# One product placed before the last of seven, first-MoE down products of two chunks in one PSUM sum, input low parts on VectorE

## The chip, the core and the metric

The kernel runs on one core of a Trainium2 chip. The metric is the device time of one execution in microseconds. Before the change the median of three runs is 1148.57 us (1141.18 to 1149.47). The execution that was profiled took 1143.19 us; its span, from the first to the last instruction, is 1141.2 us.

## What is computed

Three stages follow one another on 1536 tokens of 512 numbers (2 batches of 768 tokens, 8 heads of 64):

```
mask  = argmax(q_n . c_n) == argmax(k_n . c_n)               # cluster attention, per batch and head
x     = softmax(where(mask, q k^T / 8, -1e9)) v              # (1536, 512)
x     = (silu(x w_gate) * (x w_val)) w_out                   # first MoE: 512 -> 1536 -> 512
out   = sum over e in 0..3 of p[:, e] * (relu(x w1[e]) w2[e])  # second MoE: 512 -> 1024 -> 512, four experts
```

All of it is float32 in the reference. The kernel keeps the precision by splitting each matmul operand into a high part in the type fp32r and the float32 remainder, its low part, also in fp32r. A product of two such operands is three matmuls: high by high, high by low, low by high.

## The kernel before

**Attention** comes first (function `attention`, lines 173 to 535). Its time is not touched by the change.

**Chunks.** Both MoE stages walk over the hidden dimension in chunks of 256 columns (`FC` = 2 blocks `f` of 128). The first MoE has 6 chunks (`NC1`), the second 16 (`E2 * NC2`, four per expert). Tokens are taken in three blocks `tb` of 512.

**First MoE.** `up(key)` makes, for each block and each `f`, a gate and a value product of 12 matmuls each (`proj`, line 162), then SiLU, product, high part (ScalarE) and low part (VectorE) of the hidden tile `hh`, `hl`. `down(prev)` follows one chunk behind: 12 tiles (3 `tb` by 4 `d`) of 6 matmuls each (line 773), and after every tile VectorE adds the tile into the accumulator `acc1` in SBUF (lines 776 and 778). So the order on TensorE is up 0, up 1, down 0, up 2, down 1, and so on; down 5 runs when the second MoE begins. In the last down, ScalarE writes the high part `xh` of the second MoE's input (line 781) and GpSimd writes its low part `xl` (line 782).

**Second MoE.** `up_fast(key)` computes the first two token blocks by a scheme of seven products instead of eight (Strassen's, in Winograd's form), each product 6 matmuls (line 682), and the third token block directly, two products `g` of 12 matmuls (line 162). Some of the seven are added up in the same PSUM bank: the bank `pa` holds a product, VectorE (`add`, line 702) reads it, and then the last product is accumulated on top of it, so that the matmuls of the last product wait for VectorE's read. The sums of input blocks that the scheme needs, `x_sum(0)` to `x_sum(3)`, are made once, by the generator `x_sums` (lines 635, 636, 641), which is advanced in pieces (`side["x"]`) between the tiles of the last first-MoE down and inside the first `up_fast`. The results go through `fin` (lines 695, 696): ReLU and high part on ScalarE, low part on VectorE. `down(key)` then runs 12 tiles of 6 matmuls, taking the token tiles of block 2 first, then 1, then 0 (line 801), with the hidden tile as the stationary operand; VectorE scales by `pn` and adds to `acc2` (line 808). One chunk of the second MoE is thus 66 matmuls up and 72 down.

**Order of the work.** The whole order is written out by hand (`tc.manual_schedule()`): each engine executes its instructions in program order. Weight preparation (split into high and low parts, `w_steps`) is cut into small steps; `stage(i)` chooses the pieces for the coming chunk and `step()`, called at fixed places in `up`, `up_fast` (through `fin`) and `down`, issues some of them. A step loads the next piece through SyncE's DMA queue (`w_load`; two raw buffers), and for the second MoE four GpSimd operations make sums of weight blocks (lines 133 to 136).

**PSUM.** The up products rotate through two banks tagged `a` and two tagged `b`, the down tiles through three.

Of the kernel before, what the change touches and what calls it, by code (L numbers as in the profile page):

```python
# [7 lines left out]
F32 = mybir.dt.float32  # L8
# [5 lines left out]
ALU = mybir.AluOpType  # L14
# [21 lines left out]
def tile_cluster_attention_moe(ctx, tc, qk, vt, cent, consts, wm1, wm2, probs, out):  # L36
# [28 lines left out]
    def add_pieces(k, part):  # L65
        n = 512 if k[0] == 1 else 1024
        base, size = (0, UP[k[0]]) if part == "u" else (UP[k[0]], DN)
        pieces.extend((k, part, o, base + o) for o in range(0, size, n))

    add_pieces(chunks[0], "u")  # L70
    for i, k in enumerate(chunks):
        if k[0] == 2:
            add_pieces(k, "d")
        if i + 1 < len(chunks):
            add_pieces(chunks[i + 1], "u")
        if k[0] == 1:
            add_pieces(k, "d")
    loaded = []
    nload = [0]

# [74 lines left out]
    def proj(key, ps, base, f, tb, ks=range(4)):  # L155

        wh, wl = wt[key, "u"]
        for k in ks:
            o = base + k * FC * 128 + f * 128
            xs = (xh[:, k, tb * 512:(tb + 1) * 512], xl[:, k, tb * 512:(tb + 1) * 512])  # L160
            for m, (w, x) in enumerate(((wh, xs[0]), (wh, xs[1]), (wl, xs[0]))):
                T.matmul(out=ps, lhsT=w[:, o:o + 128], rhs=x, start=(k == 0 and m == 0), stop=(k == 3 and m == 2))  # L162
# [419 lines left out]
    def moe():  # L582
# [2 lines left out]
        ap_ = ctx.enter_context(tc.tile_pool(name="acc", bufs=1))  # L585
        tp = ctx.enter_context(tc.tile_pool(name="tp", bufs=3))
        ps_u = ctx.enter_context(tc.tile_pool(name="ps_u", bufs=2, space=PSUM))
        first_stage = ExitStack()
        hp1 = first_stage.enter_context(tc.tile_pool(name="hp1", bufs=1))
        acc = ap_.tile([128, 4 * NT], F32, tag="acc", name="acc")  # L590
        acc1 = acc.rearrange("p (d n) -> p d n", d=4)
        acc2 = acc.rearrange("p (t n) -> p t n", n=DM)
# [1 line left out]

        def stage(i):

            k = chunks[i]
            nxt = chunks[i + 1:i + 2]
            want = [(x, "u") for x in nxt]
            if k[0] == 2 or nxt[0][0] != k[0]:  # L600
                want.append((k, "d"))
            if k[0] == 1 and i:
                want.append((chunks[i - 1], "d"))
            todo = [x for x in pieces if x[:2] in want]

            def work():
                for x in todo:
                    yield from w_steps(*x[:3])

            side["work"] = work()  # L610
            side["steps"] = sum(5 if x[0][0] == 1 else 4 if x[1] == "u" else 2 for x in todo)
            side["calls"] = 7 if i == 0 else 20 if k[0] == 1 else 14

        def step():
            n = -(-side["steps"] // max(side["calls"], 1))
# [38 lines left out]

        def x_sum(i):

            if i == 0:
                return [(xh[:, j, 512:1024], xl[:, j, 512:1024]) for j in range(2)]
            return [(x_t[0][:, i - 1, j], x_t[1][:, i - 1, j]) for j in range(2)]

        def up_fast(key):

# [4 lines left out]
            def A_(f, k):  # L667
                return [(2 * k + i) * FC * 128 + f * 128 for i in range(2)]
# [7 lines left out]
            def T_(n):  # L676
                return x_sum(n - 1)
# [7 lines left out]
            def bank(tag):  # L685
                return ps_u.tile([128, 512], F32, tag=tag, name="p" + tag)
# [6 lines left out]
            def fin(f, tb, c):  # L693
                sl = slice(tb * 512, (tb + 1) * 512)
                A.activation(out=hh[:, f, sl], in_=c, func=ACTF.Relu)
                V.scalar_tensor_tensor(out=hl[:, f, sl], in0=c, scalar=0.0, in1=hh[:, f, sl].bitcast(F32),
                                       op0=ALU.max, op1=ALU.subtract)
                step()

            def add(f, tb, ps, t):  # L700
                c = tp.tile([128, 512], F32, tag="sg", name="sg")
                V.tensor_tensor(out=c, in0=ps, in1=t, op=ALU.add)  # L702
                fin(f, tb, c)
# [6 lines left out]
            for _ in range(2):  # L710
                next(side["x"], None)
            add(0, 0, pb, m1)
            for f in range(2):
                g = bank("b")
                proj(key, g, 0, f, 2)
                fin(f, 2, g)
                for _ in range(3):
                    next(side["x"], None)
            pc = bank("a")
            prod(pc, S_(1), T_(1), True)  # L720
            m5 = snap(pc)
# [3 lines left out]
            add(0, 1, pc, u2)  # L725
            prod(pa, S_(3), T_(3), False)
            add(1, 1, pa, m5)
            prod(pa, A_(1, 1), T_(4), False)
            fin(1, 0, pa)
            wt.pop((key, "u"))  # L730
# [6 lines left out]
        def up(key):  # L737
# [20 lines left out]
                    step()  # L758
            wt.pop((key, "u"))

        def down(key):
            hh, hl = h_t.pop(key)
            wh, wl = wt.pop((key, "d"))
            if key[0] == 1:
                first, last = key[1] == 0, key[1] == NC1 - 1
                for tb in range(3):
                    sl = slice(tb * 512, (tb + 1) * 512)
                    for d in range(4):
                        ps = down_banks[0].tile([128, 512], F32, tag="d", name="pd")
                        for f in range(FC):  # L770
                            o = f * DM + d * 128
                            for m, (w, x) in enumerate(((wh, hh), (wh, hl), (wl, hh))):
                                T.matmul(out=ps, lhsT=w[:, o:o + 128], rhs=x[:, f, sl],  # L773
                                         start=(f == 0 and m == 0), stop=(f == FC - 1 and m == 2))
                        if first:
                            V.tensor_copy(out=acc1[:, d, sl], in_=ps)
                        else:
                            V.tensor_tensor(out=acc1[:, d, sl], in0=ps, in1=acc1[:, d, sl], op=ALU.add)
                        if last:
                            if tb != 1 or d > 1:  # L780
                                A.copy(out=xh[:, d, sl], in_=acc1[:, d, sl])  # L781
                                G.tensor_tensor(out=xl[:, d, sl], in0=acc1[:, d, sl], in1=xh[:, d, sl].bitcast(F32), op=ALU.subtract)  # L782
                            if tb:
                                if (tb, d) == (1, 1):
                                    side["x"] = x_sums()
                                for _ in range((1 if tb == 1 else 2) if (tb, d) != (1, 0) else 0):
                                    next(side["x"], None)
                        else:
                            step()
            else:  # L790
                e = key[1] // NC2
                first, last = key[1] == 0, key[1] == E2 * NC2 - 1
                cuts = [(tb * 4 + t, slice(0, DM)) for tb in (2, 1, 0) for t in range(4)]
                if last:
                    cuts[-1:] = [(cuts[-1][0], slice(i * DM // 2, (i + 1) * DM // 2)) for i in range(2)]
                for t, cs in cuts:
                    ps = down_banks[0].tile([128, 512], F32, tag="d", name="pd")[:, cs]
                    for f in range(FC):
                        ts_ = slice(t * 128, (t + 1) * 128)
                        for m, (x, w) in enumerate(((hh, wh), (hh, wl), (hl, wh))):  # L800
                            T.matmul(out=ps, lhsT=x[:, f, ts_], rhs=w[:, f * DM + cs.start:f * DM + cs.stop],  # L801
                                     start=(f == 0 and m == 0), stop=(f == FC - 1 and m == 2))
                    pe = pn[:, t, e:e + 1]
                    y = acc2[:, t, cs]
                    if first:
                        V.tensor_scalar(out=y, in0=ps, scalar1=pe, scalar2=None, op0=ALU.mult)
                    else:
                        V.scalar_tensor_tensor(out=y, in0=ps, scalar=pe, in1=y, op0=ALU.mult, op1=ALU.add)  # L808
                    if last:
                        SY.dma_start(out=out[t * 128:(t + 1) * 128, cs], in_=y)  # L810
                    step()

        prev = None
        for i, k in enumerate(chunks):
            stage(i)
            if k[0] == 2:
                if prev is not None:
                    first_stage.close()
                    sp = ctx.enter_context(tc.tile_pool(name="sp", bufs=1))
                    x_t.extend(sp.tile([128, 3, 2, 512], F32R, name="t" + x) for x in "hl")  # L820
                    down(prev)
                    prev = None
                up_fast(k)
                down(k)
                for _ in side["work"]:
                    pass
                continue
            up(k)
            if prev is not None:
                down(prev)  # L830
            for _ in side["work"]:
                pass
            prev = k

    with tc.manual_schedule():
        attention()
# [39 lines left out]
```

## Time and profile before

| what | value |
|---|---|
| median of three runs | 1148.57 us |
| the profiled execution, and its span | 1143.19 us, 1141.2 us |
| TensorE busy, share of the span | 1071.9 us, 94% |
| VectorE, ScalarE, GpSimd busy | 751.1, 480.2, 203.4 us |
| mean granted TensorE clock | 0.978 of 2.4 GHz |
| chain that ended last | TensorE 83%, VectorE 11%, ScalarE 3% |

The chain is followed back from the last instruction, at each step to what released it. A busy TensorE is not TensorE at its peak, since the ends of matmuls are modelled (0.39 us each, while they start 0.23 us apart); the rate is read from start to start. Idle time of an engine that nobody waits for costs nothing. Attention takes the first 304 us, the first MoE runs to 586.54 us, and the second MoE from there to the end.

### The profile page before, as it was taken

Reading aid. Unit: us, or ns where it says so; the run is one execution under the profiler, and the core shown is the slowest. Engines: PE = TensorE matmul, PEld = TensorE weight load, DVE = VectorE, ACT = ScalarE, POOL = GpSimd, SP = SyncE. Lnnn points to the kernel's source line nnn. Section 1 sums busy time; section 2 is a strip of 40 time slices with the busy share of each in tenths; the row PEclk is TensorE's granted clock in tenths of the full one; section 3 lists DMA queues with packets and bytes.
Section 4 is the critical chain, followed back from the end, with each engine's and each line's share of the span. In section 5 each row is a group of like instructions: output and inputs, shape, how many; then the busy total and the mean of one; then the engine's idle time right before and its main releaser. Section 6 shows DMA issues by size and latency. Waiting matters only on the chain.

```text
span 1141.2 us, 13780 instructions
## 1 busy us (share of the span) xinstructions
PE 1071.9 (94%) x5178; PEld 898.6 (79%) x5178; DVE 751.1 (66%) x1301; ACT 480.2 (42%) x962; POOL 203.4 (18%) x192
## 2 busy tenths in 40 slices
PE   5999999999999999999989999999999999999998
PEld 3898888888888888888867777877777877777776
DVE  4798999898567566675686555555555555555554
ACT  2697888999544324243241222212222122222211
POOL 3435655442000000001051110111110111110000
PEclk9798999999999999999999999999999999999999
DMA  9666676731122121221101111001111001111002
GB/s 230 150 166 150 152 166 160 183 72 43 52 74 74 56 74 57 59 72 55 56 1 37 37 38 37 19 19 37 38 38 37 19 19 37 38 37 37 19 1 111
DMA packets 36594, 78.59 MB, mean 69 GB/s; under 512 B 16272, under 2 KB 18800, under 8 KB 36528
## 3 DMA queue, kind: packets, MB, share of 16 engines
q1 hardware_dynamic: 20256, 55.70, 17.0%
q0 software_dynamic: 16272, 22.02, 9.1%
q8 instruction: 40, 0.66, 0.2%
q14 instruction: 26, 0.21, 0.1%
HBM read 70.39 MB, written 3.19 MB: 64 GB/s over the span
## 4 chain that ended last, share of the span: by engine, by line
PE 83%; DVE 11%; ACT 3%; issue 1%; DMA 1%; SPq 0%; DVEq 0%; ACTq 0%
PE pd L801 23%; PE pb L162 16%; PE pa L682 10%; PE pd L773 8%; PE pa L162 8%; PE ps L324 5%; PE ps L300 2%; PE ps L301 2%; PE pv L342 2%; PE pv L341 2%; DVE sg L702 2%; DVE lo L332 2%; PE pb L682 2%; DVE junk L306 1%; PE pc L243 1%
## 5 line engine op out<-in xcount | busy, mean ns | idle before, releaser
L808 DVE SCALAR_TENSOR_TENSOR acc<-pd,pn,acc 128x512 f32<-128x512 f32 (+1 forms) x181 | 134.8, 747 | 93.0 <-PE pd L801 92.1
L801 PE MATMUL pd<-wdh,hh 128*128 128x512 f32 (+1 forms) x386 | 150.7, 390 | 0.0
L801 PE MATMUL pd<-wdl,hh 128*128 128x512 f32 (+1 forms) x386 | 150.5, 390 | 0.0
L801 PE MATMUL pd<-wdh,hl 128*128 128x512 f32 (+1 forms) x386 | 150.0, 389 | 0.0
L690 ACT COPY snap<-pa 128x512 f32<-128x512 f32 x48 | 28.2, 588 | 268.0 <-PE pa L682 268.0
L133 POOL TENSOR_TENSOR ws<-wraw 128x256 f32<-128x256 f32 x16 | 13.6, 852 | 649.6 <-DMA wraw<-in_wm 283.8
L332 DVE TENSOR_TENSOR lo<-ps,hi 128x384 fp32r<-128x384 f32 x192 | 101.4, 551 | 13.5 <-ACT hi L326 12.4
L162 PE MATMUL pb<-xl,wuh 128*128 128x512 f32 x264 | 103.9, 394 | 1.5 <-POOL xl L782 1.5
L162 PE MATMUL pb<-xh,wuh 128*128 128x512 f32 x264 | 103.7, 393 | 1.6 <-ACT xh L781 1.1
L324 PE MATMUL ps<-ident,P 128*128 128x128 f32 x576 | 91.5, 287 | 13.8 <-DVE lo L332 13.5
L162 PE MATMUL pb<-xh,wul 128*128 128x512 f32 x264 | 103.6, 392 | 0.0
L306 DVE CUSTOM_DVE_ANT_1 junk<-ps,zero 128x768 bf16<-128x768 f32 x96 | 90.9, 947 | 13.2 <-PE ps L301 12.5
L326 ACT CAST hi<-ps 128x384 fp32r<-128x384 f32 x192 | 85.8, 483 | 28.0 <-PE ps L324 25.8
L318 ACT ACTIVATE P<-ps,nm 128x768 f32<-128x768 f32 x96 | 87.3, 909 | 14.5 <-DVE nm L306 13.4
L324 PEld LDWEIGHTS ps<-ident,P 128*128 128x128 f32 x576 | 69.6, 146 | 28.7 <-DVE lo L332 21.8
L801 PEld LDWEIGHTS pd<-wdh,hh 128*128 128x128 f32 x386 | 73.3, 190 | 15.3
L801 PEld LDWEIGHTS pd<-wdl,hh 128*128 128x128 f32 x386 | 73.1, 189 | 15.3
L801 PEld LDWEIGHTS pd<-wdh,hl 128*128 128x128 f32 x386 | 73.0, 189 | 15.2
L341 PE MATMUL pv<-hi,vs 128*128 128x384 f32 x192 | 74.2, 386 | 0.0
L300 PE MATMUL ps<-t 80*128 80x384 f32 x192 | 72.3, 377 | 0.5 <-ACT P L318 0.4
L682 PE MATMUL pa<-th,wuh 128*128 128x512 f32 x96 | 40.9, 426 | 32.8 <-DVE sg L702 32.8
L301 PE MATMUL ps<-t 128*128 128x384 f32 x192 | 67.8, 353 | 0.0
(159 smaller groups left out, 2316.5 us busy)
## 6 DMA issues: line engine op xcount, KB each, us to landing
wraw<-in_wm SPq DMA_DIRECT2D x68, 512.0 KB, 3.7
t<-in_qk POOLq DMA_DIRECT2D x15, 768.0 KB, 5.5
t<-in_qk POOLq DMA_DIRECT2D x18, 384.0 KB, 6.8
raw<-in_qk SPq DMA_DIRECT2D x32, 192.0 KB, 7.0
x<-x SPq DMA_DIRECT2D x21, 192.0 KB, 4.8
vs<-in_vt POOLq DMA_DIRECT2D x16, 192.0 KB, 3.8
vraw<-in_vt SPq DMA_DIRECT2D x16, 192.0 KB, 3.8
R<-rd SPq DMA_DIRECT2D x16, 192.0 KB, 3.5
```

Source lines behind the costliest of these rows:

```text
L162: T.matmul(out=ps, lhsT=w[:, o:o + 128], rhs=x, start=(k == 0 and m == 0), stop=(k == 3 and m == 2))
L300: T.matmul(out=ps, lhsT=t2[:, 0, qs], rhs=t2[:, 1, ks], start=True, stop=False)
L301: T.matmul(out=ps, lhsT=t1[:, 0, qs], rhs=t1[:, 1, ks], start=False, stop=True)
L306: V.tensor_tensor_reduce(out=junk.rearrange("p (c n) -> p c n", c=2), in0=S_t[n][:, :, :384], in1=zero1.rearrange("p (o n) -> p o n", o=1) ...
L318: A.activation(out=P_t[n].rearrange("p (c n) -> p c n", c=2), in_=S_t.pop(n)[:, :, :384], func=ACTF.Exp, scale=0.125, bias=nm_t.pop(n), ac ...
L324: T.transpose(ps[:, i * 128:(i + 1) * 128], P_t[3 * u + i][:, j * 128:(j + 1) * 128], ident)
L332: V.tensor_tensor(out=lo, in0=ps, in1=hi.bitcast(F32), op=ALU.subtract)
L341: T.matmul(out=pv_t[u], lhsT=lhsT, rhs=hi, start=(j == 0), stop=False)
L682: T.matmul(out=ps, lhsT=w[:, o:o + 128], rhs=r, start=first and i == 0 and m == 0, stop=i == 1 and m == 2, skip_group_check=not first)
L773: T.matmul(out=ps, lhsT=w[:, o:o + 128], rhs=x[:, f, sl], start=(f == 0 and m == 0), stop=(f == FC - 1 and m == 2))
L801: T.matmul(out=ps, lhsT=x[:, f, ts_], rhs=w[:, f * DM + cs.start:f * DM + cs.stop], start=(f == 0 and m == 0), stop=(f == FC - 1 and m == 2))
L808: V.scalar_tensor_tensor(out=y, in0=ps, scalar=pe, in1=y, op0=ALU.mult, op1=ALU.add)
```

## The change

There are three parts.

1. In `up_fast`, the third block's product for `f` = 1 is issued after the sixth of the seven products and its `add`, and before the last. Before, both products of the third block stood together ahead of the products of sums.
2. In the first MoE, the down products of two chunks (0 and 1, 2 and 3, 4 and 5) are done together, by `down_pair`, after the second one's `up`: one PSUM tile takes 12 matmuls, 6 of each chunk, and VectorE adds once per tile. The order of the weight pieces and the number of steps per call follow.
3. In the last pair the low parts `xl` are made by VectorE, one tile behind, instead of by GpSimd. The input sums are stored in the hidden tile of chunk 4, which is read block by block, instead of in a tile of their own, and the generator is advanced at somewhat other places.

```
@@ order of weight pieces
         if k[0] == 2:
             add_pieces(k, "d")
+        elif k[1] % 2:
+            add_pieces(chunks[i - 1], "d")
+            add_pieces(k, "d")
         if i + 1 < len(chunks):
             add_pieces(chunks[i + 1], "u")
-        if k[0] == 1:
-            add_pieces(k, "d")
@@ stage
-            nxt = chunks[i + 1:i + 2]
-            want = [(x, "u") for x in nxt]
-            if k[0] == 2 or nxt[0][0] != k[0]:
+            want = [(x, "u") for x in chunks[i + 1:i + 2]]
+            if k[0] == 2:
                 want.append((k, "d"))
-            if k[0] == 1 and i:
-                want.append((chunks[i - 1], "d"))
+            elif k[1] % 2:
+                want += [(x, "d") for x in chunks[i - 1:i + 1]]
...
-            side["calls"] = 7 if i == 0 else 20 if k[0] == 1 else 14
+            side["calls"] = 7 if i == 0 else 14 if k[0] == 2 else 10 if k[1] % 2 == 0 or k[1] == NC1 - 1 else 20
@@ x_sum
-            return [(x_t[0][:, i - 1, j], x_t[1][:, i - 1, j]) for j in range(2)]
+            tb = (None, 1, 0, 2)[i]
+            return [[t[:, j, tb * 512:(tb + 1) * 512] for t in x_t] for j in range(2)]
@@ up_fast
             add(0, 0, pb, m1)
-            for f in range(2):
-                g = bank("b")
-                proj(key, g, 0, f, 2)
-                fin(f, 2, g)
-                for _ in range(3):
-                    next(side["x"], None)
+            g = bank("b")
+            proj(key, g, 0, 0, 2)
+            fin(0, 2, g)
+            for _ in range(2):
+                next(side["x"], None)
             pc = bank("a")
             prod(pc, S_(1), T_(1), True)
...
             prod(pa, S_(3), T_(3), False)
             add(1, 1, pa, m5)
+            g = bank("b")
+            proj(key, g, 0, 1, 2)
+            fin(1, 2, g)
             prod(pa, A_(1, 1), T_(4), False)
             fin(1, 0, pa)
@@ the first MoE's part of down() becomes
+        def down_pair(keys):
+            first, last = keys[0][1] == 0, keys[1][1] == NC1 - 1
+            hs, ws = [h_t.pop(k) for k in keys], [wt.pop((k, "d")) for k in keys]
+            if last:
+                x_t.extend(hs[0])
+            terms = [(w, x, f) for (hh, hl), (wh, wl) in zip(hs, ws) for f in range(FC)
+                     for w, x in ((wh, hh), (wh, hl), (wl, hh))]
+            low = None
+            for tb in range(3):
+                sl = slice(tb * 512, (tb + 1) * 512)
+                for d in range(4):
+                    ps = down_banks[0].tile([128, 512], F32, tag="d", name="pd")
+                    y = acc1[:, d, sl]
+                    for n, (w, x, f) in enumerate(terms):
+                        o = f * DM + d * 128
+                        T.matmul(out=ps, lhsT=w[:, o:o + 128], rhs=x[:, f, sl], start=(n == 0), stop=(n == len(terms) - 1))
+                    if first:
+                        V.tensor_copy(out=y, in_=ps)
+                    else:
+                        V.tensor_tensor(out=y, in0=ps, in1=y, op=ALU.add)
+                    if last:
+                        if low:
+                            V.tensor_tensor(out=low[0], in0=low[1], in1=low[2].bitcast(F32), op=ALU.subtract)
+                            low = None
+                        if tb != 1 or d > 1:
+                            A.copy(out=xh[:, d, sl], in_=y)
+                            low = xl[:, d, sl], y, xh[:, d, sl]
+                        if (tb, d) == (1, 1):
+                            side["x"] = x_sums()
+                        for _ in range(1 if tb == 1 and d < 3 else 2):
+                            next(side["x"], None)
+                    step()
+            if low:
+                V.tensor_tensor(out=low[0], in0=low[1], in1=low[2].bitcast(F32), op=ALU.subtract)
@@ main loop
-            up(k)
-            if prev is not None:
-                down(prev)
+            else:
+                up(k)
+                if k[1] % 2:
+                    down_pair(chunks[i - 1:i + 1])
```

## Rows read from the trace of the kernel before

**Rows 1.** Page, part 1: busy us, share of the span, instructions of each engine.

```profile
PE 1071.9 (94%) x5178; PEld 898.6 (79%) x5178; DVE 751.1 (66%) x1301; ACT 480.2 (42%) x962; POOL 203.4 (18%) x192
```

**Rows 2.** Windows: stretch, length, busy PE, PEld, DVE, ACT, POOL (count), PEclk, DMA, GB/s.

```profile
304.00:574.00 270.00, 270.00 (x1193) 223.58 (x1192) 176.08 (x297) 98.50 (x172) 4.03 (x5) 1.00 0.21 65
585.00:590.00 5.00, 5.00 (x24) 4.14 (x23) 5.00 (x6) 3.02 (x5) 2.95 (x3) 1.00 0.00 0
586.54:606.68 20.14, 17.05 (x61) 12.39 (x59) 16.93 (x23) 9.59 (x17) 8.47 (x7) 0.83 0.08 27
586.54:1137.46 550.92, 515.04 (x2215) 419.44 (x2213) 310.00 (x443) 138.21 (x243) 52.31 (x63) 0.98 0.10 33
846.22:881.46 35.24, 33.15 (x139) 27.02 (x139) 19.07 (x27) 8.51 (x16) 2.92 (x4) 0.95 0.09 30
```

**Rows 3.** Waits of PE after 300 us: who for whom, total, times, longest.

```profile
PE pa L682 <- DVE sg L702: 32.8, 16, 2.1
```

**Rows 4.** Chain of waits, second chunk of the second MoE: start, us, what.

```profile
642.58 1.66 PE pa L682 x6
644.24 16.32 PE pd L801 x72
```

**Rows 5.** Timeline of PE and PEld, same chunk, last product: start, us, instruction [idle].

```profile
640.11 0.39 PE L682 MATMUL pa<-th,wul 128*128 128x512 f32 x1
...
642.58 0.19 PEld L682 LDWEIGHTS pa<-th,wuh 128*128 128x128 f32 x1 [2.51 <-DVE sg L702]
...
642.58 0.50 PE L682 MATMUL pa<-th,wuh 128*128 128x512 f32 x1 [2.09 <-DVE sg L702]
642.92 0.39 PE L682 MATMUL pa<-tl,wuh 128*128 128x512 f32 x1
```

**Rows 6.** Timeline of DVE and ACT, same chunk, end of the seven products.

```profile
641.84 0.68 DVE L702 TENSOR_TENSOR sg<-pa,snap 128x512 f32<-128x512 f32 x1
643.22 0.69 DVE L696 SCALAR_TENSOR_TENSOR hl<-sg,hh 128x512 fp32r<-128x512 f32 x1 [0.70 <-ACT hh L695]
643.83 0.68 DVE L152 TENSOR_TENSOR wul<-ws,wuh 128x512 fp32r<-128x512 f32 x1
...
642.56 0.63 ACT L695 ACTIVATE hh<-sg 128x512 fp32r<-128x512 f32 x1 [1.45 <-DVE sg L702]
643.10 0.60 ACT L151 CAST wuh<-ws 128x512 fp32r<-128x512 f32 x1
```

**Rows 7.** Timeline of PE: first matmul after the wait, four of sixteen chunks.

```profile
608.92 0.50 PE L682 MATMUL pa<-th,wuh 128*128 128x512 f32 x1 [2.09 <-DVE sg L702]
...
846.18 0.78 PE L682 MATMUL pa<-th,wuh 128*128 128x512 f32 x1 [2.09 <-DVE sg L702]
846.76 0.63 PE L682 MATMUL pa<-tl,wuh 128*128 128x512 f32 x1
847.19 0.63 PE L682 MATMUL pa<-th,wul 128*128 128x512 f32 x1
...
881.42 0.50 PE L682 MATMUL pa<-th,wuh 128*128 128x512 f32 x1 [2.09 <-DVE sg L702]
...
1119.58 0.50 PE L682 MATMUL pa<-th,wuh 128*128 128x512 f32 x1 [1.49 <-DVE sg L702]
```

**Rows 8.** Groups of DVE, 304 to 574 us: shapes, count, busy us, mean ns, idle.

```profile
L778 DVE TENSOR_TENSOR acc<-pd,acc 128x512 f32<-128x512 f32 x50 | 34.4, 688 | 10.3 <-PE pd L773 9.4
```

**Rows 9.** Single lines: count, ns min/median/max, first to last start.

```profile
L782 POOL TENSOR_TENSOR xl<-acc,xh x10: 1290/1408/1649, 573.2 to 593.2; 128x512 fp32r<-128x512 f32 x10
...
L635 DVE TENSOR_TENSOR t<-acc,t x4: 675/1212/1778, 584.8 to 593.5; 128x512 f32<-128x512 f32 x4
...
L641 DVE TENSOR_TENSOR tl<-t,th x6: 676/678/1769, 590.1 to 601.0; 128x512 fp32r<-128x512 f32 x6
```

**Rows 10.** Timeline, last up of the first MoE: tenth step's last operation; first down matmul.

```profile
550.72 0.68 DVE L152 TENSOR_TENSOR wul<-ws,wuh 128x512 fp32r<-128x512 f32 x1
...
553.90 0.39 PE L773 MATMUL pd<-hh,wdh 128*128 128x512 f32 x1
```

More of the change, by code (lines that the diff above doesn't have):

```diff
@@ L587, in moe @@
         ps_u = ctx.enter_context(tc.tile_pool(name="ps_u", bufs=2, space=PSUM))
-        first_stage = ExitStack()
-        hp1 = first_stage.enter_context(tc.tile_pool(name="hp1", bufs=1))
+        hp1 = ctx.enter_context(tc.tile_pool(name="hp1", bufs=1))
         acc = ap_.tile([128, 4 * NT], F32, tag="acc", name="acc")
@@ L763, in down @@
             wh, wl = wt.pop((key, "d"))
[L764 to L793, printed above, removed]
-                if last:
[L795 to L811, printed above, removed]
@@ L813, in moe @@
-        prev = None
+            e = key[1] // NC2
+            first, last = key[1] == 0, key[1] == E2 * NC2 - 1
+            cuts = [(tb * 4 + t, slice(0, DM)) for tb in (2, 1, 0) for t in range(4)]
+            if last:
+                cuts[-1:] = [(cuts[-1][0], slice(i * DM // 2, (i + 1) * DM // 2)) for i in range(2)]
+            for t, cs in cuts:
+                ps = down_banks[0].tile([128, 512], F32, tag="d", name="pd")[:, cs]
+                for f in range(FC):
+                    ts_ = slice(t * 128, (t + 1) * 128)
+                    for m, (x, w) in enumerate(((hh, wh), (hh, wl), (hl, wh))):
+                        T.matmul(out=ps, lhsT=x[:, f, ts_], rhs=w[:, f * DM + cs.start:f * DM + cs.stop],
+                                 start=(f == 0 and m == 0), stop=(f == FC - 1 and m == 2))
+                pe = pn[:, t, e:e + 1]
+                y = acc2[:, t, cs]
+                if first:
+                    V.tensor_scalar(out=y, in0=ps, scalar1=pe, scalar2=None, op0=ALU.mult)
+                else:
+                    V.scalar_tensor_tensor(out=y, in0=ps, scalar=pe, in1=y, op0=ALU.mult, op1=ALU.add)
+                if last:
+                    SY.dma_start(out=out[t * 128:(t + 1) * 128, cs], in_=y)
+                step()
@@ L816, in moe @@
             if k[0] == 2:
-                if prev is not None:
-                    first_stage.close()
-                    sp = ctx.enter_context(tc.tile_pool(name="sp", bufs=1))
-                    x_t.extend(sp.tile([128, 3, 2, 512], F32R, name="t" + x) for x in "hl")
-                    down(prev)
-                    prev = None
                 up_fast(k)
                 down(k)
-                for _ in side["work"]:
-                    pass
-                continue
-            up(k)
-            if prev is not None:
-                down(prev)
+            else:
+                up(k)
+                if k[1] % 2:
+                    down_pair(chunks[i - 1:i + 1])
             for _ in side["work"]:
                 pass
-            prev = k
     with tc.manual_schedule():
```

## The prediction

> **What bounds the kernel now.** The page comes first: TensorE is busy 94% of the span, no other engine over 66% [rows 1]. That is a mean over stages, so I cut the time with the windows. From 304 to 574 us, the first MoE, TensorE is busy for every one of 270.00 us at a granted clock of 1.00 [rows 2]. Nothing but fewer matmuls can shorten that stretch, and the change keeps their number. The second MoE, 586.54 to 1137.46 us, is different: clock 0.98 and 36 us without a matmul [rows 2]. The list of waits names the place: 16 waits of the bank `pa` on VectorE's `sg`, 32.8 us, one per chunk, at the last of the seven products [rows 3]. The chain and the timeline of one chunk show it: the sixth product's last matmul starts at 640.11, the seventh's first at 642.58, when VectorE has read `pa` at 641.84 + 0.68 = 642.52 [rows 5, 6].
>
> What the second MoE would take without waits comes from start to start: 72 down matmuls in 16.32 us [rows 4] are 0.2267 us each. 16 chunks of 66 + 72 are 2208 matmuls, 500.5 us. It takes 550.9 [rows 2], so 50.4 us are lost, in four terms:
> - the waits, 32.8 us [rows 3];
> - the restart behind each: six matmuls in 1.66 us [rows 4] where 1.36 would do, 16 x 0.30 = 4.8 us;
> - the clock: behind some waits the matmuls start 0.43 us apart, the 1.2 GHz level, as from 846.76 to 847.19, and the way to the next wait is then 35.24 us instead of 33.66 [rows 7]. The 15 intervals from first to last wait take 510.66 us, 5.8 over 15 x 33.66, with the last wait 0.6 us shorter [rows 7]: 6.4 us, four such drops of 1.58 us;
> - the first `up_fast`: its 60 matmuls ahead of its wait take 20.14 us [rows 2] instead of 13.6, 6.5 us.
>
> The sum is 50.5, as it should be.
>
> **Part 1, the product moved.** It removes nothing and adds nothing: 12 matmuls, one ReLU, one low part and two weight steps go behind the sixth product. They fill the wait. The last of the sixth product's matmuls gives way at 640.34; the 12 take 2.72 us, so the last product comes at 643.06. VectorE is through with `pa` at 642.52, 0.54 us earlier, and it has the same work in front of it as now: one `hl`, one weight split, then the add [rows 6]. (The sums on GpSimd are issued one step later; they wait for nobody on this path, and GpSimd has 52 us of work in 551 [rows 2]; the load that SyncE's queue issues with a weight step goes about 2.6 us later, for data wanted a chunk later.) So all 16 waits go, with the restarts and the clock drops that stand behind them: 32.8 + 4.8 + 6.4 = 44.0 us.
>
> The restart is counted as the rows have it: the last product's first weight load starts with its matmul, at 642.58, after 2.51 us of idleness, and the next matmul follows 0.34 us on instead of 0.23 [rows 5]. A rule of the Trainium skill has it otherwise: "TensorE: Matmul & The Clock Gate" (Engine queue depths) lets TensorE pull weight loads ahead of matmuls in flight. By the rule the load would be done within the wait, and 16 x 0.11 = 1.8 us less could be gained; the trace decides against it here.
>
> What is late next: `down` begins with the third block, and its sixth matmul takes as weights the low part of `f` = 1, which is now made last. The 12 moved matmuls end at about 643.22 (start 642.83, 0.39 each). ScalarE then has the ReLU of 642.56 and the cast of 643.10 before it [rows 6], so the new ReLU runs from about 643.62 to 644.22. VectorE has the low part of 643.22 and the split of 643.83 before it [rows 6], so the new low part runs from 644.43 to 645.12. `down` begins at 643.06 + 1.36 = 644.42, its sixth matmul at 645.55, the load a little earlier, at 645.33: spare 0.2 us. That is thin. I take it as free, and keep for the range 16 times a lateness of up to 0.5 us and a restart of 0.3 (as behind today's wait): 13 us. On the good side there is no bound beyond zero. After that VectorE clears the first down tile at about 647.6, and the bank is wanted by the fourth tile at 648.5.
>
> **Part 2, the pairs.** VectorE loses 36 of 72 evictions of 0.688 us [rows 8], 25 us, all under a TensorE that never waits [rows 2]: zero. What could be lost is the cover. Before, a chunk's down weights were ready an `up` ahead; now both chunks' 20 steps run inside the second `up`, done by its tenth of twelve calls. That call's last operation ends at 551.4 where the `up` ends at 553.90 [rows 10]; the second chunk's `f` = 1 is wanted 9 matmuls, 2.0 us, later still. Spare 4.5 us; in the last pair, at three steps a call, the eighth call is the last. Zero again. SyncE's queue carries the same loads in another order.
>
> **Part 3, the first `up_fast`.** Before, VectorE is the bound there: 5.00 us of 5.00 [rows 2]. Per tile of 1.36 us it has an eviction and two pieces of the sums, starts 0.60 us apart at best, 1.8 us; and pieces that read SBUF twice stretch from 0.68 to 1.77 us while GpSimd makes a low part of 1.4 us [rows 9]. After, tiles are 2.72 us, and per tile VectorE has an eviction, a low part, two pieces: 2.4 us. When the last tile ends, eviction, low part, two pieces, low part remain, 3.2 us; the direct product wants the last low part 22 matmuls, 5.0 us, later. Spare 1.8 us. So the 6.5 us go too; the nearest bound is that they stay, and 10 more operations of 0.60 us come on top.
>
> A page of the Trainium skill speaks against this part: "Perfetto Trace Analysis" (Optimizing Scalar/DVE Operations) says that if VectorE is saturated, offloading to ScalarE or even GpSimd may make sense, and adds that the two share a port. By its first half the stretch would get longer, up to 6.5 + 6.0 us; by the second half the offload was no help, which the stretched rows bear out.
>
> **The sum.** 44.0 + 6.5 = 50.5 us off the profiled 1143.2 gives 1092.7. That execution is 5.4 us faster than the median shown, 2.0 slower than the fastest run. If the others differ by more clock drops behind waits, the median falls to the same 1093; if the difference comes from attention, to 1098. I take 1094, a little residue included.
>
> **Rivals.**
> - *The wait moves to down's first tile.* For it: a spare of 0.2 us by rows of another order. Against: the chain is the same six operations. 1094 + 5 to 13 us, 1099 to 1107. Chance 0.14.
> - *VectorE stays the bound at the first `up_fast`.* For it: it is full there. Against: the tiles are twice as long. 1094 + 6.5, up to 12.5 with the added operations: 1100 to 1106. Chance 0.07.
> - *The change doesn't do what it says:* the last product waits for something later than the read of `pa`, such as the low part of the fourth sum, so the waits stay. Against: the wait is put down to `sg` 16 times of 16. Only 6.5 us go: 1142 against the median. Chance 0.03.
> - *Slower: the clock.* TensorE would be unbroken for 550 us. If its clock then fell to the lower level by itself, each microsecond there would cost 1 - 0.2267/0.43 = 0.47 us. The gain is used up at 107 us of it, and the time is 1% above before from 132 us of the second MoE's 500: 1160. Against: 270 us without a gap at 1.00 [rows 2], with drops only behind waits. Chance 0.03.
>
> **Numbers.** The forecast has 0.73: 1090 to 1098. The range takes in the first two rivals, and below the fastest run's 2 us: 1089 to 1107. A measurement of this kernel can tell 1%, 11.5 us, from no change. Faster takes the forecast and the first two rivals, 0.94; same the third, 0.03; slower the fourth, 0.03.
>
> **What would show it.** Right: no wait of `pa` on `sg` in the second MoE, chunks 31.3 us apart, clock 1.00 from 304 us to the end, TensorE full around the first `up_fast`, and the first MoE's end unmoved at about 586.5. Wrong: a wait of `pd` on `hl` or `hh` (first rival), of `pb` on `xl` (second), of `pa` still on VectorE (third), or a low clock without a wait in front (fourth). A wait of `pd` on weights in the first MoE would sink part 2.

## Result

The changed kernel takes 1093.19 us, the median of four runs (1088.62 to 1104.27); the kernel before takes 1145.63 (1141.18 to 1149.47, four runs: the three ahead of the prediction and one beside the changed kernel). The ratio is 0.956, with a 95% interval of 0.948 to 0.964: faster by 4.4%. The profiled execution took 1092.93 us with a span of 1090.9, where the sum of the prediction was 1092.7.

The page of the changed kernel, part 1, against [rows 1]: TensorE is at 97%, VectorE has lost 28 us of work, GpSimd 17.

```profile
PE 1057.6 (97%) x5178; PEld 893.2 (82%) x5178; DVE 723.5 (66%) x1275; ACT 476.6 (44%) x962; POOL 186.5 (17%) x182
```

The windows of the changed kernel, with the columns of [rows 2]: the same stretch of the first MoE, the first 60 matmuls of the first `up_fast`, and the whole second MoE.

```profile
304.00:574.00 270.00, 270.00 (x1193) 223.57 (x1192) 161.86 (x272) 100.68 (x176) 4.02 (x4) 1.00 0.21 65
586.65:600.25 13.60, 13.60 (x61) 11.26 (x60) 11.64 (x18) 7.02 (x13) 4.03 (x4) 1.00 0.12 40
586.65:1087.23 500.58, 500.58 (x2215) 414.67 (x2213) 297.63 (x437) 132.75 (x239) 44.16 (x60) 1.00 0.11 36
```

The second MoE takes 500.58 us instead of 550.92 [rows 2], and all of the 50.3 us by which the span is shorter come from there. TensorE is busy in every one of these microseconds at a granted clock of 1.00. The list of TensorE's waits after 300 us, which held 32.8 us for `pa` [rows 3], is empty. The first MoE begins and ends where it did: VectorE has 14 us less to do in the window of 270 us, and the time is the same.

The chain of waits in the second chunk, against [rows 4]: it consists of TensorE alone, and the last product (6 matmuls) takes 1.36 us, no longer 1.66.

```profile
629.00 2.72 PE pb L163 x12
631.72 1.36 PE pa L684 x6
633.08 16.32 PE pd L814 x72
```

The timeline of VectorE, TensorE and the weight loads in that chunk, against [rows 5, 6]: the read of `pa` (L704), three operations after it the new low part (`hl<-pb`), the last product's first matmul, down's first and sixth, and the loads of the last product's first and of down's sixth.

```profile
630.35 0.68 DVE L704 TENSOR_TENSOR sg<-pa,snap 128x512 f32<-128x512 f32 x1
631.73 0.69 DVE L698 SCALAR_TENSOR_TENSOR hl<-sg,hh 128x512 fp32r<-128x512 f32 x1 [0.70 <-ACT hh L697]
632.34 0.68 DVE L143 TENSOR_TENSOR wul<-wraw,wuh 128x512 fp32r<-128x512 f32 x1
632.94 0.68 DVE L698 SCALAR_TENSOR_TENSOR hl<-pb,hh 128x512 fp32r<-128x512 f32 x1
...
631.56 0.39 PE L684 MATMUL pa<-hh,wuh 128*128 128x512 f32 x1
...
632.92 0.39 PE L814 MATMUL pd<-wdh,hh 128*128 128x512 f32 x1
...
634.05 0.39 PE L814 MATMUL pd<-wdh,hl 128*128 128x512 f32 x1
...
631.33 0.19 PEld L684 LDWEIGHTS pa<-hh,wuh 128*128 128x128 f32 x1
...
633.83 0.19 PEld L814 LDWEIGHTS pd<-wdh,hl 128*128 128x128 f32 x1
```

VectorE has read `pa` at 631.03, and the last product's first matmul starts at 631.56: 0.53 us to spare, that is, between the end of the work waited for and the start that needs it. The weight load of that matmul waits for the same read [rows 5], and it starts at 631.33: counted there, the spare is 0.30 us. The low part is done at 633.62, and its load starts at 633.83: 0.21 us to spare.

The two lines of the input sums in the changed kernel, with the columns of [rows 9]: no operation is stretched any more.

```profile
L635 DVE TENSOR_TENSOR t<-acc,t x4: 683/684/689, 579.9 to 588.7; 128x512 f32<-128x512 f32 x4
...
L641 DVE TENSOR_TENSOR hl<-t,hh x6: 680/683/686, 585.3 to 596.0; 128x512 fp32r<-128x512 f32 x6
```

### The profile page after: what moved, and what is told of

It reads as the page before. It is cut to its first block, busy times and chain, and to the rows that moved or that the text cites. A ratio compares the mean times of both kernels' runs of the same rounds, so it can differ in the third digit from the quotient of the medians.

```text
span 1090.9 us, 13739 instructions
## 1 busy us (share of the span) xinstructions
PE 1057.6 (97%) x5178; PEld 893.2 (82%) x5178; DVE 723.5 (66%) x1275; ACT 476.6 (44%) x962; POOL 186.5 (17%) x182
## 4 chain that ended last, share of the span: by engine, by line
PE 89%; DVE 6%; ACT 2%; DMA 1%; issue 1%; SPq 0%; ACTq 0%; DVEq 0%
PE pd L814 24%; PE pb L163 16%; PE pa L684 12%; PE pd L781 9%; PE pa L163 8%; PE ps L325 5%; PE ps L301 2%; PE ps L302 2%; PE pv L342 2%; PE pv L343 2%; DVE lo L333 2%; PE pb L684 2%; DVE junk L307 1%; DMA raw<-in_qk 1%; PE pc L244 1%; PE pu L163 1%
## 5 line engine op out<-in xcount | busy, mean ns | idle before, releaser
L319 ACT ACTIVATE P<-ps,nm 128x768 f32<-128x768 f32 x96 | 87.4, 911 | 15.7 <-DVE nm L307 14.4
L343 PE MATMUL pv<-lo,vs 128*128 128x384 f32 x192 | 65.4, 341 | 0.0
```

What stands on the lines that cost most here:

```text
L319: A.activation(out=P_t[n].rearrange("p (c n) -> p c n", c=2), in_=S_t.pop(n)[:, :, :384], func=ACTF.Exp, scale=0.125, bias=nm_t.pop(n), ac ...
```

## Experiments

The measure is the length of the second MoE, from the first matmul of the first `up_fast` to the end of the last matmul (put 0.12 us after its start, since the last ones, of half width, start 0.12 us apart). Before it is 550.92 us, after 500.58. The theory is the one of the prediction: waits with their restarts and clock drops, 44.0 us, and the first `up_fast`, 6.5 us. Whole times are given too, but attention, which no kernel here changes, moves them by more than some of the effects (see the end of this section).

### Part 1 alone

```
 # before.py, up_fast
-            for f in range(2):
-                g = bank("b")
-                proj(key, g, 0, f, 2)
-                fin(f, 2, g)
-                for _ in range(3):
-                    next(side["x"], None)
+            g = bank("b")
+            proj(key, g, 0, 0, 2)
+            fin(0, 2, g)
+            for _ in range(3):
+                next(side["x"], None)
...
             add(1, 1, pa, m5)
+            g = bank("b")
+            proj(key, g, 0, 1, 2)
+            fin(1, 2, g)
```

> Part 1 alone, on the kernel before: the third block's second product goes behind the sixth product, nothing else. Theory (16 waits of pa with restarts and clock drops are 44.0 us, the first up_fast 6.5 us of its own): the second MoE takes 550.9 - 44.0 = 506.9 us, the execution about 1099; TensorE still stops in the first up_fast, for 6.5 us in all. Rival (the parts need each other, since a late VectorE in the first up_fast or the thin spare at down's first tile costs more without the pairs): above 510 us.

Measured: 1100.85 us (four runs, 1094.17 to 1104.12), 0.962 of before (0.956 to 0.967). The window of its second MoE, and TensorE's waits after 300 us:

```profile
591.63:1098.67 507.04, 503.14 (x2215) 415.43 (x2213) 303.44 (x443) 135.27 (x243) 48.66 (x63) 1.00 0.11 36
```

```profile
PE pb L162 <- POOL xl L784: 1.5, 2, 1.2
PE pa L682 <- DVE tl L641: 1.3, 1, 1.3
PE pb L162 <- ACT xh L783: 1.1, 1, 1.1
```

507.04 where 506.9 was expected. The 16 waits are gone, and what is left stands in the first `up_fast`: the low and high parts of the input come late there, and so does one low part of a sum (`tl`). Part 1 is worth 43.9 of the 50.3 us, and needs neither of the other parts.

### Parts 2 and 3 alone

```
 # after.py, up_fast: the product back at its old place
             fin(0, 2, g)
             for _ in range(2):
                 next(side["x"], None)
+            g = bank("b")
+            proj(key, g, 0, 1, 2)
+            fin(1, 2, g)
...
             add(1, 1, pa, m5)
-            g = bank("b")
-            proj(key, g, 0, 1, 2)
-            fin(1, 2, g)
```

> Parts 2 and 3 without part 1: the changed kernel with the third block's two products side by side again, ahead of the products of sums. Theory: only the 6.5 us of the first up_fast go, the 16 waits stay with restarts and drops: second MoE 544.4 us, execution about 1137. Rival (halving the evictions of the first MoE is worth something on the path): the first MoE shorter than 286.5 us from the first MoE's start to the first up_fast, or the second MoE below 543.

Measured: 1138.18 us (ten runs, 1133.16 to 1146.51), 0.995 of before (0.992 to 0.999). TensorE's waits after 300 us, and the second MoE:

```profile
PE pa L684 <- DVE sg L704: 32.8, 16, 2.1
```

```profile
586.40:1132.49 546.09, 513.31 (x2215) 419.20 (x2213) 304.01 (x437) 135.77 (x239) 47.23 (x60) 0.98 0.10 33
```

The first `up_fast` runs through, and the 16 waits of 2.09 us (the last 1.49) are back to the tenth. The second MoE is 1.7 us longer than expected: five of the intervals from wait to wait are 35.2 to 35.3 us long instead of 33.66, where before has three such and a fourth drop in its last interval (34.66 us, with the shorter last wait in it). Each drop costs 1.6 us. With that the sum closes: 500.5 + 32.8 + 4.8 + 5 x 1.58 = 546.0. The first MoE is no shorter: from its last early matmul (the last of those of the first chunk that the program issues inside attention, tile `pu`) at 303.30 to the first `up_fast` at 586.40 it is 283.10 us, to the hundredth what the kernel before takes from 303.44 to 586.54. The 36 evictions saved are worth nothing there.

### The low parts on GpSimd again, with the pairs

```
 # after.py, down_pair
                         if tb != 1 or d > 1:
                             A.copy(out=xh[:, d, sl], in_=y)
-                            low = xl[:, d, sl], y, xh[:, d, sl]
+                            G.tensor_tensor(out=xl[:, d, sl], in0=y, in1=xh[:, d, sl].bitcast(F32), op=ALU.subtract)
```

(and the two places that issue `low` on VectorE go.)

> The changed kernel with the low parts of the input on GpSimd again, right behind their high part. Theory (the doubled tile time of the pairs is what makes room, not the engine): the last low part is ready 0.7 + 0.6 + 1.5 = 2.8 us after the last tile, wanted 5.0 us after it, and VectorE has 1.8 us of work in 2.7 per tile even if stretched by the shared reads: second MoE 500.5 to 502 us. Rival (the move to VectorE is what takes the wait away): TensorE stops for several us in the first up_fast, second MoE about 507.

Measured: 1088.36 us, one run. Its second MoE, and the last low part on GpSimd:

```profile
582.33:1082.88 500.55, 500.55 (x2215) 414.68 (x2213) 297.38 (x435) 132.72 (x239) 46.40 (x62) 1.00 0.11 36
```

```profile
583.95 1.64 POOL L788 TENSOR_TENSOR xl<-acc,xh 128x512 fp32r<-128x512 f32 x1 [1.09 <-ACT xh L787]
```

And the low parts of the input sums on VectorE:

```profile
L641 DVE TENSOR_TENSOR hl<-t,hh x6: 676/680/1797, 580.4 to 591.6; 128x512 fp32r<-128x512 f32 x6
```

500.55: no wait. The last low part is done 3.3 us after the first `up_fast` has begun, and is wanted 5.0 us after it. One of VectorE's operations is stretched again, to 1.797 us, and nothing waits for it. With pairs it does not matter which engine makes the low parts. (The changed places of the generator and of the stored sums are in this kernel as well; what they do without the pairs was not tried. The whole time is 4.6 us below the changed kernel's profiled one because attention ended 4.3 us earlier.)

### The low parts on VectorE, without the pairs

```
 # before.py, down, first MoE
                         if last:
+                            if low:
+                                V.tensor_tensor(out=low[0], in0=low[1], in1=low[2].bitcast(F32), op=ALU.subtract)
+                                low = None
                             if tb != 1 or d > 1:
                                 A.copy(out=xh[:, d, sl], in_=acc1[:, d, sl])
-                                G.tensor_tensor(out=xl[:, d, sl], in0=acc1[:, d, sl], in1=xh[:, d, sl].bitcast(F32), op=ALU.subtract)
+                                low = xl[:, d, sl], acc1[:, d, sl], xh[:, d, sl]
```

> Part 3 alone: the kernel before, with only the low parts of the input moved to VectorE, one tile behind; single down chunks, both products side by side. Theory (VectorE is full there but no longer stretched): from the second tile of the middle block on VectorE has 24 operations of 0.60 us, 14.4 us, from 8.0 us ahead of the last tile's end, so it is through 6.4 us after it; the direct product wants the last low part 5.0 us after it and the next bank follows: 3 to 5 us lost in place of 6.5, second MoE 547 to 549 us. Rival (a saturated VectorE must not be given more): 10 operations of 0.60 us longer, the 60 matmuls take up to 26 us, second MoE 551 to 557.

Measured: 1140.56 us, one run. The first 60 matmuls of the first `up_fast`, the second MoE, and the sums' line on VectorE:

```profile
582.10:600.50 18.40, 15.85 (x61) 11.90 (x59) 15.74 (x25) 8.70 (x16) 3.66 (x4) 0.91 0.09 29
582.10:1134.53 552.43, 517.10 (x2215) 421.17 (x2213) 308.66 (x445) 137.31 (x242) 47.29 (x60) 0.98 0.10 33
```

```profile
L635 DVE TENSOR_TENSOR t<-acc,t x4: 683/684/684, 580.5 to 588.9; 128x512 f32<-128x512 f32 x4
```

The stretch takes 18.40 us instead of 20.14: 4.8 us are lost there instead of 6.5, inside the 3 to 5 expected. Ten more operations on a VectorE that was already full made the stretch shorter, since the others are no longer stretched (0.684 us each, where they had gone up to 1.778 [rows 9]).

Not all of the 1.74 us is VectorE's. The last wait of the stretch, for the first sum `sg`, ends at 596.55 before and at 590.84 here; behind it 36 matmuls run without a wait, before and here:

```profile
596.55:606.68 10.13, 10.12 (x36) 8.02 (x36) 6.96 (x10) 4.78 (x9) 3.21 (x4) 0.81 0.16 53
```

```profile
590.84:600.50 9.66, 9.66 (x36) 7.73 (x36) 7.06 (x10) 4.78 (x9) 3.23 (x4) 0.85 0.17 56
```

Up to that point it is 10.01 us before and 8.74 here, 1.27 us less, with VectorE at work without a pause in both. The other 0.47 us lie behind it, where the clock is at its 1.2 GHz level for less of the time. 36 matmuls at the full clock are 8.2 us, so of the 6.5 us lost before some 2.0 lie behind the last wait, clock and restart, and 4.6 up to it, VectorE's lateness.

The length of the whole second MoE, 552.43, missed the expectation of 547 to 549, and lies in the rival's range, but not by the rival's mechanism: six clock drops instead of four. 500.5 + 4.8 + 32.8 + 4.8 + 6 x 1.58 = 552.4. I had not allowed for the number of drops to change.

### The spare at down's sixth matmul

```
 # after.py, fin: for the moved product the weight step goes ahead of the low part
                 A.activation(out=hh[:, f, sl], in_=c, func=ACTF.Relu)
+                if (f, tb) == (1, 2):
+                    step()
                 V.scalar_tensor_tensor(out=hl[:, f, sl], in0=c, scalar=0.0, in1=hh[:, f, sl].bitcast(F32),
                                        op0=ALU.max, op1=ALU.subtract)
-                step()
+                if (f, tb) != (1, 2):
+                    step()
```

> The changed kernel with one swap in every second-MoE chunk: the weight step that followed the moved product's low part on VectorE now precedes it, so that low part comes 0.60 us later. Theory (0.2 us of spare at down's sixth matmul): a wait of pd on the low part of about 0.4 us in each of 15 or 16 chunks, with a restart of 0.1 to 0.3 us: second MoE 500.6 + 8 to 11 = 508 to 512 us; no clock drops, since the clock fell in the runs so far only behind waits of 1 us or more. Rival (TensorE has more room there than the rows say): second MoE unchanged at 500.6.

Measured: 1098.60 us, one run. TensorE's waits, the second MoE, and two of the matmuls behind the wait:

```profile
PE pd L817 <- DVE hl L700: 5.8, 15, 0.5
```

```profile
581.71:1092.87 511.16, 505.33 (x2215) 413.56 (x2213) 300.13 (x437) 132.78 (x239) 44.22 (x60) 1.00 0.10 36
```

```profile
662.45 0.50 PE L817 MATMUL pd<-wdh,hl 128*128 128x512 f32 x1 [0.38 <-DVE hl L700]
...
694.40 0.50 PE L817 MATMUL pd<-wdh,hl 128*128 128x512 f32 x1 [0.38 <-DVE hl L700]
```

Down's first and fifth matmul in the third chunk, the weight step's operation on VectorE, the low part behind it, and the load that waits for it:

```profile
660.78 0.39 PE L817 MATMUL pd<-wdh,hh 128*128 128x512 f32 x1
...
661.11 0.69 DVE L153 TENSOR_TENSOR wul<-ws,wuh 128x512 fp32r<-128x512 f32 x1 [0.22 <-ACT wuh L152]
...
661.68 0.39 PE L817 MATMUL pd<-wdl,hh 128*128 128x512 f32 x1
661.72 0.68 DVE L700 SCALAR_TENSOR_TENSOR hl<-pb,hh 128x512 fp32r<-128x512 f32 x1
...
662.45 0.19 PEld L817 LDWEIGHTS pd<-wdh,hl 128*128 128x128 f32 x1 [0.80 <-DVE hl L700]
```

There are 15 waits, 0.38 us each but the first (0.54). The low part comes 0.92 us later, not 0.60: it ends 0.70 us after the start of down's first matmul in the changed kernel (632.92, 633.62) and 1.62 us after it here (660.78, 662.40), because VectorE also stands 0.22 us until ScalarE's cast of the weight step is done. Its load, which started with down's fifth matmul, starts 0.77 us behind it, so some 0.15 of the 0.92 us was spare, in line with the 0.2 of the rows. The last chunk has no weight step at that place and no wait. Two chunks stand 31.95 to 32.00 us apart, with 31.28 us of matmuls: a wait of 0.38 costs 0.67 to 0.72. The clock stays at 1.00. The first rival of the prediction is thus real and one small step away: one weight step put before that low part costs 10.6 us.

### Half of the product

```
 # after.py, up_fast
             fin(0, 2, g)
...
+            g = bank("b")
+            proj(key, g, 0, 1, 2, range(2))
             pc = bank("a")
...
             add(1, 1, pa, m5)
-            g = bank("b")
-            proj(key, g, 0, 1, 2)
+            proj(key, g, 0, 1, 2, range(2, 4))
             fin(1, 2, g)
```

> The changed kernel with the third block's second product cut in two: its first 6 matmuls at the old place, only the last 6 behind the sixth product. Theory (VectorE is through 2.2 us after the sixth product, 6 matmuls cover 1.36 us of it): 0.9 us per chunk from start to start remain, with up to 0.3 us of restart, 16 times 0.9 to 1.2: second MoE 515 to 520 us, and up to 524 if the clock drops come back. Rival (any cover at all is enough, or none short of the whole): 500.6, or 544 us.

Measured: 1115.34 us, one run. TensorE's waits, the second MoE, and two of the matmuls behind the wait:

```profile
PE pa L684 <- DVE sg L704: 10.9, 15, 0.7
```

```profile
591.91:1109.69 517.78, 506.75 (x2215) 412.28 (x2213) 297.46 (x437) 132.54 (x239) 44.13 (x60) 1.00 0.10 35
```

```profile
638.80 0.50 PE L684 MATMUL pa<-hh,wuh 128*128 128x512 f32 x1 [0.73 <-DVE sg L704]
...
671.20 0.50 PE L684 MATMUL pa<-hh,wuh 128*128 128x512 f32 x1 [0.73 <-DVE sg L704]
```

517.78, in the range of 515 to 520. 1.36 us of cover shorten the wait by exactly 1.36, from 2.09 to 0.73; the chunk is 32.40 us instead of 33.66. The cover, the work that TensorE does meanwhile, counts microsecond for microsecond. The sixteenth wait, 1.49 us before [rows 7], is down to 0.13 and too short for the list. How little cover would do was not tried; by the 0.30 us that the weight load has to spare in the changed kernel, an estimate is 11 of the 12 matmuls. There is no clock drop behind any of these waits.

### Where the runs differ

The eight profiled executions of the eight kernels differ ahead of the second MoE, in attention, whose function is the same in all of them. The first `up_fast` begins earliest, at 581.71, in the run with the weight step before the low part, and latest, at 591.91, in the one with half of the product. A line of attention in the two, with its first and last start:

```profile
L325 PE MATMUL ps<-ident,P x576: 270/273/421, 34.8 to 291.5; 128*128 128x128 f32 x192
```

```profile
L325 PE MATMUL ps<-ident,P x576: 270/273/474, 45.1 to 301.7; 128*128 128x128 f32 x192
```

That is 10.2 us. From the last early matmul to the first `up_fast` it is 283.10 us in each (298.61 to 581.71, 308.81 to 591.91), so all of it lies in attention, and between these two it is there from the first start of that line on, 34.8 against 45.1 us. Over the first 50 us the granted clock is 0.97 in the one and 0.88 in the other, but the clock alone does not order the eight: over the first 300 us it is 0.95 in the kernel before, 0.97 in the latest and 0.98 in the earliest. The cause was not tried and stays open.

## Why the prediction was right

- **The account of the second MoE** held to the tenth. 2208 matmuls were put at 500.5 us, and they take 500.58. The terms were checked in two groups: part 1 alone takes 43.9 us away (44.0 predicted for waits, restarts and clock drops), and parts 2 and 3 alone leave the 32.8 us of waits as they were. The lengths with full waits are the sum of the same terms once the clock drops of the execution are counted; their number, which the prediction took from one trace, is four to six.
- **The restart** of 0.30 us has the right total, since a chunk with the wait is 2.38 us longer than one without it (33.66 against 31.28). But some 0.16 of the 0.30 is wait: the profile has the matmul ahead busy for 0.39 us, where the next would start after 0.23. And the prediction's remark that the trace decides against weight loads being pulled ahead goes too far: the load's own row shows it waiting 2.51 us for `sg` [rows 5], so it shows nothing of a load that has nothing left to wait for.
- **Cover of the wait.** A spare of 0.54 us was predicted and 0.53 is there, counted at the matmul (0.30 at its load); half of the cover, 1.36 us, leaves 0.73 us of the 2.09.
- **The next thing that is late,** the low part at down's sixth matmul, was named with 0.2 us of spare, and has 0.21. It was taken as free, which was right; with the swapped step, a low part 0.92 us later costs 10.6 us, within the first rival's 5 to 13.
- **Part 2** was costed at nothing on its own, and is worth nothing on its own in the first MoE. What it gives is room in front of the first `up_fast`: the tiles of the last pair take 2.72 us instead of 1.36.
- **Part 3** was a term of the right size with the credit not divided. The 6.5 us go, but the move to VectorE isn't what takes them: with pairs GpSimd does as well, and without pairs the stretch is 1.7 us shorter, 1.27 by VectorE and 0.47 behind the last wait, by the clock. The prediction also put all of the 6.5 us down to VectorE, where some 2.0 were clock and restart. By the Trainium skill's advice to take work off a saturated VectorE ("Perfetto Trace Analysis", Optimizing Scalar/DVE Operations) moving work back onto it would have made the stretch longer, and it became shorter. The trace goes with the same paragraph's warning of a shared port, and with "SBUF — State Buffer" (Who interferes with whom), by which a VectorE operation with two SBUF inputs contends with a GpSimd operation that reads SBUF: such operations took up to 1.778 us beside GpSimd [rows 9] and 0.684 without it, while the evictions of the kernel before, with one input in PSUM, stayed at 0.692 us or less in the very stretch in which GpSimd made the low parts:

```profile
L778 DVE TENSOR_TENSOR acc<-pd,acc x10: 676/692/692, 573.1 to 588.4; 128x512 f32<-128x512 f32 x10
```

- **The offset to the median** was the weak step. The prediction put the 5.4 us between profiled execution and median down to clock drops, or else to attention, and took the first. The drops do vary, four to six among the three profiled executions with full waits, 3 us in all; but attention varies by 10 us, and the changed kernel, without a wait, still spreads over 15.7 us. Thirteen later runs of the kernel before spread over 14 us, 1138.57 to 1152.62, with granted clocks of 0.983 in the fastest and 0.981 in the slowest, so the clock is the smaller part of it. That the median came within 1 us of the forecast is owed in part to which runs were drawn.

## What to carry over

Where one engine is to be full, count what a stage would take at the spacing of its own instructions and account for every microsecond above that; when the terms close, the gain of a reordering can be told closely. What missed here, by 1.7 and 3 us in two experiments, was the number of clock drops. A wait for a read of PSUM is best filled with independent work of at least the same length, and the next operand that becomes late should be looked for at once: here it had 0.2 us, and one weight step in front of it gives back a fifth of the gain. Halving the work of an engine nobody waits for is worth nothing, except at the place where it is the bound.

## What was not expected of the hardware

A wait of TensorE costs more than the list of waits shows. From start to start, 0.38 us in the list made a chunk 0.67 to 0.72 us longer, 0.73 made it 1.12 longer (32.40 against 31.28), and 2.09 made it 2.38 longer (33.66). The surplus, 0.3 to 0.4 us, hardly depends on the length, so short waits are dear. About 0.16 of it is the way of counting named above. Another 0.11 is a slower start: the second matmul behind the wait follows at 0.34 us instead of 0.23 [rows 5]. In the run with half of the product 0.08 more is lost at down's sixth matmul (673.83, the next at 674.13).

In the three profiled executions with full waits (before, parts 2 and 3 alone, part 3 alone) the clock fell to the 1.2 GHz level behind 4, 5 and 6 of the 16 waits, 1.6 us each time; behind 15 waits of 0.38 us and 15 of 0.73 us, one in a chunk, it never fell. In the first `up_fast` of the kernel before and of part 3 alone it fell among waits of 0.3 to 1.2 us that stood close together (granted clock 0.83 [rows 2] and 0.91). The number changes between executions of the same waits, so a comparison of whole times carries a few microseconds of it.
